# Two instruction counts in the model that orders a windowed-attention and gated-MLP kernel

## The chip, the cores and the metric

One core of one Trainium2 chip runs the whole kernel as one launch. The metric is the device time of one execution in microseconds; the time before is the median of three runs. The core has TensorE (PE, with its weight loads PEld), VectorE (DVE), ScalarE (ACT), GpSimd (POOL) and SyncE (SP, which issues nearly all DMAs here). Each engine works through its own list of instructions in order and waits on semaphores.

## What is computed

Attention over 8 batches and 8 heads of 576 tokens, with a window of 32 (heads 0 to 3) or a dilated window of 128 with step 4 (heads 4 to 7), and then a gated MLP on the 4608 tokens:

```python
scores = scale * np.matmul(q, k.transpose(0, 1, 3, 2))       # (8, 8, 576, 576), D = 64
mask_plain = (rel >= 0) & (rel < window)
mask_dil = (rel >= 0) & (rel < window * dilation) & (rel % dilation == 0)
attn = softmax(np.where(masks, scores, -1e9))
x = np.matmul(attn, v)                                       # to (4608, 512)
h = x @ w_in                                                 # (512, 2048)
out = (h * (1.0 / (1.0 + np.exp(-1.702 * h)))) @ w_out       # (2048, 512)
```

## The kernel before

**Work and stages.** Heads are taken in pairs: pair k is batch k // 4 and heads 2 (k % 4) and the next, so pairs 0 to 3 are batch 0 and pairs 2 and 3 of a batch are dilated. The first four pairs ("early" pairs) have a form of their own: `first_attention` (scores and softmax), `first_transposed` and `first_multiplied` (the product with v). The MLP is computed with every operand split into a high and a low part, in three matmuls for each product. Three groups (m0, m1, m2: the tokens of batches 0 to 2) go through `Group.up` and `Down`: for each of 16 chunks f of the hidden width, 12 matmuls into a bank `hp_m_f`, a tanh on ScalarE (line 855), a gating step on VectorE (line 856) that frees the bank, a copy to the high part `gh` (line 346), a subtraction to the low part `gl` (line 353), and 8 matmuls with `gh` (lines 784 and 785) and 4 with `gl` (line 788) into four accumulators `acc`. Three blocks of two groups each (p, q, r) then go through `up_` and `second_` matmuls (lines 992 and 1107). Each execution also decodes the weights, which come as 64-bit words, into high and low parts (`decode`): for each of the 32 pieces wi0 to wi15 and wo0 to wo15 a DMA of 512 KB and eight steps on ScalarE, VectorE and GpSimd (lines 396 to 406, 346, 353). This runs beside group m0.

**What sets the order.** The program doesn't write out an order. Each piece of work is handed to a `Plan` by `add`, with the engines that may run it and a cost on each, an urgency, what it reads and writes, and, for some pieces on TensorE, a `count`: the instructions that the piece has there. `Plan.placed` plays the program through with those costs: it takes, again and again, the engine that can start soonest and on it the most urgent piece, and chooses among engines that may run a piece. `Plan.ordered` does so four times, with due times worked out from the round before. The list that comes out is the order of every engine's instructions; the modelled times themselves are thrown away, and each piece then starts when its semaphores let it.

**The count.** `fetched` in `placed` holds that TensorE's program arrives in blocks of 256 instructions: the first edge is at instruction 193, the next ones at 449, 705, 961, 1217 and 1473, and nothing past instruction 1500 is modelled. At an edge the modelled engine waits until the next block is there, 4.2 or 6.1 us after it got to the edge before. Only pieces before instruction 1500 are moved by it directly; those are the four early pairs' scores and products, and the first matmuls of group m0.

**Fillers.** While `when < WARM` (60 us), the plan fills TensorE's modelled idle time with matmuls that nobody reads: 128x512 ones of bf16 (line 1249, two instructions each), and, before the next edge in the first 25 us, small ones (line 1253, four instructions each):

```python
small = min((193 + 256 * (len(blocks) - 1) - issued[0]) // 4 + 1, int((when - at - 0.1) / 0.045))
idle = max(0, int((when - max(at, 1.5) - 0.5) / size))
```

Their number hangs on the modelled idle time and on the instructions counted so far.

Of the kernel before, what the change touches and what calls it, by code (L numbers as in the profile page):

```python
# [43 lines left out]
PE, ACT, DVE, POOL, DMA = range(5)  # L44
# [4 lines left out]
class Plan:  # L49
# [9 lines left out]
    def add(self, costs, urgency, work, reads=(), writes=(), slack=0.0, count=0):  # L59

        i, after = len(self.ops), set()
        for k in reads:
            after.add(self.writer.get(k))  # L70
        for k in writes:
            after.add(self.writer.get(k))
            after.update(self.readers.get(k, ()))
        for k in writes:
            self.writer[k], self.readers[k] = i, []
        for k in reads:
            if k not in writes:
                self.readers.setdefault(k, []).append(i)
        self.ops.append((costs, (urgency, i), work, after - {None, i}, slack, count))
# [138 lines left out]
def tile_windowed_attention_then_gated_mlp(  # L218
# [19 lines left out]
    add = plan.add  # L238
# [7 lines left out]
    def bank(shape, tag, name):  # L246
        return ps.tile(shape, F32, tag=tag, name=name)
# [169 lines left out]
    FOUR = tuple(f"acc{j}" for j in range(NC))  # L417

    def lots(k):

        if 0 < k < NC:
            return f"first qk{k}", f"first v{k}"
        return "qk0", "v0"

    def load_qk(k):
        u, place = pairs[k], lots(k)[0]

        def work(e):
            if 0 < k < NC:
                flat = (None, late, main_x, left_x)[k]  # L430
            else:
                flat = temp([P, 2 * S], F32, "qk", f"qk_{k}")

            u["qk"] = flat[:, 0:2 * S]
            load(u["qk"], qk[k])

        add({DMA: 590}, (-9.0, -5.7, -4.7, -2.3)[k] if k < NC else 1.6 * k - 2.0, work, waits(k), (place, place + "l"))

    def load_v(k):
        u, place = pairs[k], lots(k)[1]  # L440

        def work(e):
            if k < NC:
                n = (QT if dilated(k) else QT + 1) * 2 * D
                flat = (None, late, main_x, left_x)[k][:, 2 * S:2 * S + n] if k else temp([P, n], F32, "v", f"v_{k}")
                u["v"] = flat.rearrange("p (s a d) -> p s a d", a=2, d=D)

                load(flat, first_v[k][:, 2 * D * (QT + 1) - n:])
                return
            flat = temp([P, 2 * NB * D], F32, "v", f"v_{k}")  # L450
            u["v"] = flat.rearrange("p (a s d) -> p a s d", a=2, s=NB)
            load(flat, vp[k - NC])

        add({DMA: 390 if k < NC else 328}, (-6.7, -6.7, -3.8, -1.6)[k] if k < NC else 1.6 * k - 0.3, work, waits(k),
            (place, place + "l"), (0.0, 4.0, 11.0, 14.0)[k] if k < NC else 0.0)
# [5 lines left out]
    def dilated(k):  # L461
        return k % NC >= NC // 2

    def turn(k):
        return k % (3 if FIRST * NC <= k < INNER else 2)

    def masked(k):

        return k < FIRST * NC

    def scores(k):
        u = pairs[k]
        u["sp"] = bank([P, 2, GT], "sp", f"sp_{k}")
        u["all"] = u["sp"][:, :, 0:QT * W].rearrange("p a (t w) -> p a t w", t=QT)
        u["box"] = [u["all"][:, a] for a in range(2)]
        if masked(k):
            for a in range(2):
                T.matmul(u["box"][a], ident, plain if not dilated(k) else classes if k < NC else mask, start=True,
                         stop=False, skip_group_check=True)
        for t in range(QT):  # L480
            for a, g in [(a, g) for a in range(2) for g in range(4 if k < NC or t < QT - 1 else 2)]:
                rows = slice(D * a, D * a + D)
                dst = u["box"][a][32 * g:32 * g + 32, t]
                at = ROW * g + 32 * t if k < NC else MID * (g % 2) + W * t + 32 * (g // 2)

                spans = [(0, W, at - 32)]
                if at + 32 > S:
                    spans = [(0, S + 32 - at, at - 32), (S + 32 - at, at + 32 - S, 0)]
                for w, n, first in spans:
                    T.matmul(dst[:, w:w + n], u["qk"][rows, at:at + 32], u["qk"][rows, S + first:S + first + n],  # L490
                             start=not masked(k), stop=True, tile_position=(D * a, 32 * g), skip_group_check=True)
# [28 lines left out]
    def softmax(k, urgency):  # L520

        y = turn(k)
        pr, sm, ct = prs[y], sms[y], cts[y]
        PR, SM, CT = (f"{n}{y}" for n in ("pr", "sm", "ct"))
        exponentials(k, urgency)
        add({DVE: 0.81}, urgency, lambda e: V.tensor_reduce(out=sm, in_=sets[y], axis=AX.X, op=ALU.add), (PR,), (SM,))
        inverse(k, urgency)
        for a in range(2):
            add({POOL: 0.85, DVE: -0.48}, urgency, lambda e, a=a: pair(
                e, pr[:, a], pr[:, a], sm[:, a, :, None].broadcast_to([P, QT, W]), ALU.mult), (SM,), (f"{PR}.{a}",))  # L530
        if k < NC:
            return
        for half in (0, 1):
            add({DVE: 0.42}, urgency, lambda e, half=half: V.transpose(  # L534
                out=ct[:, half].rearrange("p t a q -> p a t q"), in_=pr[:, :, :, 32 - 32 * half:64 - 32 * half]),
                (PR, f"{PR}.0", f"{PR}.1"), (f"{CT}.{half}",))

        for m in range(8):  # L540
            j, prev = m % 4, m // 4
            upper, second = j % 2, j in (1, 2)
            row = D * upper + 32 * (second != prev)
            col = 32 if second else 64 * prev
            tiles = slice(1 if j == 0 and prev else 0, QT - j // 2)
            to = slice(1, QT) if j == 3 and not prev else slice(0, tiles.stop - tiles.start)
            dst = bt[row:row + 32, to, :, col:col + 32]
            src = ct[32 * j:32 * j + 32, prev, tiles]

            def work(e, dst=dst, src=src):  # L550
                if e == DMA:
                    load(dst, src)
                else:
                    copy(e, dst, src)

            costs = {DMA: 82} if k < FIRST * NC else {ACT: 0.49, DVE: -0.33}
            add(costs, urgency, work, (f"{CT}.{prev}",), (f"bt.{m}",))

    def first_product(k):

        u = pairs[k]
        ct = cts[turn(k)].rearrange("p h t a q -> p (h t a q)").rearrange("p (a n) -> p a n", a=2)
        u["x"] = first_x[:, :, ROW * (k % 2):ROW * (k % 2) + ROW]
        for s in range(QT + 1):
            at, to = max(W * s // 2 - 32, 0), min(32 * s + 32, ROW)

            n = max(W * s - 32, 0)  # L570
            for g in range(4):
                if s == 0 and (g == 0 or dilated(k)):
                    continue
                for a in range(2):
                    T.matmul(u["x"][D * a:D * a + D, g, at:to],
                             u["v"][32 * g:32 * g + 32, s - 1 if dilated(k) else s, a],
                             ct[32 * g:32 * g + 32, a, n:n + to - at],
                             start=s == 0 or s == 1 and (g == 0 or dilated(k)), stop=s == QT, tile_position=(32 * g, D * a), skip_group_check=True)
# [88 lines left out]
    def first_attention(k):  # L667


        load_qk(k)  # L670
        load_v(k)
        add({PE: 1.5 if k else 2.3}, k - 1.0e5, lambda e: scores(k), (lots(k)[0],), ("sp", f"scores{k}"), count=180)
        softmax(k, k)

    def first_transposed(k):
# [5 lines left out]
    def first_multiplied(k):  # L681


        y = turn(k)
        add({PE: 1.4}, k - 1.0e5, lambda e: first_product(k), (lots(k)[1], f"ct{y}.0", f"ct{y}.1", f"scores{NC - 1}"),
            FOUR, count=184)
        drain_x(k, k)

    def attention(k, urgency):
# [516 lines left out]
    for c in range(NC):  # L1206
        first_attention(c)
        if c < 2:
            first_transposed(c)
        if c in (1, 2):  # L1210
            decode(c - 1, c + 1.3)
    for c in range(NC):
        first_multiplied(c)
        if c < 2:
            first_transposed(c + 2)
# [88 lines left out]
```

## Time and profile before

| | |
|---|---|
| median of 3 runs | 823.08 us (820.47 to 823.29) |
| the profiled execution, own time | 822.47 us |
| its span | 820.7 us |
| mean granted clock of TensorE | 0.999 of 2.4 GHz |
| PE busy | 806.5 us (98%) |
| PEld busy | 653.1 us (80%) |
| DVE, ACT, POOL busy | 665.0, 514.5, 330.5 us (81, 63, 40%) |

The sums below are made against the profiled execution's 822.47 us: the span of 820.7 us from its first to its last instruction, and 1.8 us around it. It lies 0.6 us under the median of the three runs. Matmuls overlap in the trace (one of 512 columns is shown for 0.39 us, and the next starts 0.23 us after it), so a busy PE may hide short waits; the idle time of PEld, and what ended it, shows them.

### The profile page before, as it was taken

How to read it: one execution, taken by the hardware profiler on the slowest of the kernel's cores; microseconds unless marked ns; L12 is line 12 of the kernel's file. 1: busy time of each engine (PE TensorE's matmuls, PEld its weight loads, DVE VectorE, ACT ScalarE, POOL GpSimd, SP SyncE). 2: the span in 40 equal slices, each digit the busy share in tenths (PEclk: the TensorE clock that was granted, in tenths of full speed). 3: DMA queues.
4: the chain of work that ended last, by engine and by line, in shares of the span. 5: the costliest groups of instructions: out<-in, count | busy, mean ns of one | idle time of the engine just before them, and what ended most of it. 6: DMA issues, size and time to landing. Idle time of an engine off the chain costs nothing.

```text
span 820.7 us, 18907 instructions
## 1 busy us (share of the span) xinstructions
PE 806.5 (98%) x7279; PEld 653.1 (80%) x7279; DVE 665.0 (81%) x1083; ACT 514.5 (63%) x982; POOL 330.5 (40%) x297
## 2 busy tenths in 40 slices
PE   7999999999999999999999999999999999999997
PEld 4677787888888888878888888888788888888886
DVE  6799989778788787798888999986679885867575
ACT  7998985667677767587766754556356534544340
POOL 3443417555746663222334555531215332112250
PEclk9999999999999999999999999999999999999999
DMA  9577659889667656796877878776565658675546
GB/s 354 172 242 211 182 176 302 289 287 317 201 213 251 201 190 228 251 314 229 264 251 252 284 217 287 234 255 187 174 207 189 204 185 278 201 223 158 178 151 182
DMA packets 109610, 188.13 MB, mean 229 GB/s; under 512 B 26448, under 2 KB 55376, under 8 KB 109520
## 3 DMA queue, kind: packets, MB, share of 16 engines
q1 hardware_dynamic: 109376, 186.78, 69.9%
q8 instruction: 58, 0.95, 0.5%
q14 instruction: 32, 0.26, 0.1%
q10 hardware_dynamic: 144, 0.13, 0.0%
HBM read 140.64 MB, written 45.09 MB: 226 GB/s over the span
## 4 chain that ended last, share of the span: by engine, by line
PE 90%; DVE 4%; DMA 3%; ACT 1%; issue 1%; SPq 0%; DVEq 0%; ACTq 0%
PE hp_m L847 14%; PE up_r L992 9%; PE up_q L992 9%; PE up_p L992 9%; PE second_p_Q L1107 5%; PE second_q_Q L1107 5%; PE second_r_Q L1107 5%; PE acc_m L784 5%; PE acc_m L788 5%; PE acc_m L785 5%; PE sp L490 3%; PE second_r_Z L1107 3%; PE second_p_Z L1107 3%; PE second_q_Z L1107 3%; PE second_R L1107 3%; PE av L593 2%
## 5 line engine op out<-in xcount | busy, mean ns | idle before, releaser
L353 POOL TENSOR_TENSOR arena<-arena 128x256 f32<-128x256 f32 (+3 forms) x96 | 99.5, 1051 | 131.7 <-DVE wo_kept L353 27.4
L847 PE MATMUL hp_m<-xs,wi_kept 128*128 128x512 f32 x504 | 128.6, 396 | 0.9 <-DVE arena L856 0.7
L847 PEld LDWEIGHTS hp_m<-xs,wi_kept 128*128 128x128 f32 x504 | 92.8, 188 | 22.8 <-DVE arena L856 2.2
L353 POOL TENSOR_TENSOR wo_kept<-arena,wo_kept 128x512 fp32r<-128x512 f32 x35 | 47.4, 1359 | 128.0 <-ACT wo_kept L346 90.3
L346 ACT ACTIVATE wo_kept<-arena 128x512 fp32r<-128x512 f32 x114 | 71.2, 630 | 39.6 <-PE second_r_Q L1107 11.0
L992 PE MATMUL up_r<-wi_kept,xs 128*128 128x512 f32 x336 | 85.3, 389 | 0.0
L992 PE MATMUL up_p<-wi_kept,xs 128*128 128x512 f32 x336 | 85.2, 391 | 0.0
L992 PE MATMUL up_q<-wi_kept,xs 128*128 128x512 f32 x336 | 84.1, 389 | 0.0
L992 PEld LDWEIGHTS up_r<-wi_kept,xs 128*128 128x128 f32 x336 | 63.1, 188 | 13.1
L992 PEld LDWEIGHTS up_q<-wi_kept,xs 128*128 128x128 f32 x336 | 63.1, 188 | 13.1
L992 PEld LDWEIGHTS up_p<-wi_kept,xs 128*128 128x128 f32 x336 | 62.7, 188 | 13.4
L353 POOL TENSOR_TENSOR wo_kept<-wi_last_units,wo_kept 128x512 fp32r<-128x512 f32 x26 | 35.9, 1380 | 86.1 <-ACT wo_kept L346 77.5
L353 DVE TENSOR_TENSOR wo_kept<-arena,wo_kept 128x512 fp32r<-128x512 f32 x86 | 62.4, 734 | 6.7 <-ACT wo_kept L346 6.0
L784 PE MATMUL acc_m<-gh,wo_kept 128*128 128x512 f32 x156 | 62.1, 398 | 0.6 <-ACT arena L346 0.5
L785 PE MATMUL acc_m<-gh,wo_kept 128*128 128x512 f32 x156 | 60.9, 391 | 0.0
L1013 ACT ACTIVATE arena<-arena 128x512 f32<-128x512 f32 x60 | 37.6, 628 | 34.9 <-DVE arena L353 30.5
L346 ACT ACTIVATE bt<-ct 32x256 f32<-32x256 f32 (+1 forms) x125 | 54.4, 435 | 7.2 <-DVE ct L534 3.9
L353 DVE TENSOR_TENSOR arena<-arena 128x512 f32<-128x512 f32 (+1 forms) x75 | 56.3, 756 | 2.8 <-ACT arena L346 1.7
L353 POOL TENSOR_TENSOR pr<-pr,sm 128x320 f32<-128x320 f32 x52 | 43.5, 849 | 26.4 <-DVE sm L518 22.6
L353 DVE TENSOR_TENSOR gl<-arena,gh 128x512 fp32r<-128x512 f32 x52 | 43.5, 836 | 7.5 <-PE acc_m L788 3.4
L346 ACT ACTIVATE wo_kept<-wi_last_units 128x512 fp32r<-128x512 f32 x48 | 30.2, 629 | 27.9 <-PE second_r_Z L1107 8.6
L1014 DVE SCALAR_TENSOR_TENSOR arena<-arena 128x512 f32<-128x512 f32 x60 | 46.6, 781 | 1.0 <-ACT arena L1013 0.5
(261 smaller groups left out, 1850.2 us busy)
## 6 DMA issues: line engine op xcount, KB each, us to landing
xs<-sums SPq DMA_DIRECT2D x168, 256.0 KB, 3.3
out_weights<-sums_o SPq DMA_DIRECT2D x63, 512.0 KB, 3.8
qk<-qk_dram SPq DMA_DIRECT2D x29, 576.0 KB, 4.3
xs<-sums_o SPq DMA_DIRECT2D x21, 512.0 KB, 3.5
v<-vp_dram SPq DMA_DIRECT2D x28, 320.0 KB, 4.3
sums<-arena SPq DMA_DIRECT2D x32, 256.0 KB, 3.1
sums_o<-arena SPq DMA_DIRECT2D x32, 256.0 KB, 3.0
arena<-wi_dram SPq DMA_DIRECT2D x15, 512.0 KB, 5.3
```

Of the source, the lines that this page charges most:

```text
L346: A.activation(dst, src, AF.Copy, scale=scale)
L353: (V if e == DVE else G).tensor_tensor(out=dst, in0=a, in1=b, op=op)
L490: T.matmul(dst[:, w:w + n], u["qk"][rows, at:at + 32], u["qk"][rows, S + first:S + first + n], start=not masked(k), stop=True, tile_positi ...
L593: T.matmul(u["x"][i][rows, at:at + last - first], u["v"][keys, a, m], bt[keys, m, a, first:last], start=(i, a) not in begun, stop=True, ti ...
L784: T.matmul(self.acc[j], w[:, 0, cols], high, start=f == 0, stop=False)
L785: T.matmul(self.acc[j], w[:, 1, cols], high, start=False, stop=False)
L788: T.matmul(self.acc[j], w[:, 0, P * j:P * j + P], low, start=False, stop=f == NF - 1)
L847: T.matmul(hps[f], wi(f)[:, st, cols], mv[:, c], start=c == 0 and k == 0, stop=c == NC - 1 and k == 2)
L992: T.matmul(self.banks[place], xs[:, slot, at:at + P], wi_kept[:, 2 * a + c, mv], start=fresh and c == 0 and k == 0, stop=c == 1 and k == 2 ...
L1013: add({ACT: 0.60}, -10.0, lambda e: A.activation(unit(tmp), src(), AF.Tanh, scale=0.851), need, own(tmp))
L1014: add({DVE: -0.70 if need[0][0] == "A" else 0.70}, -10.0, lambda e: V.scalar_tensor_tensor(out=unit(dst), in0=unit(tmp), scalar=1.0, in1=s ...
L1107: T.matmul(self.second[key], w[:, st, cols], mv, start=fresh and y == 0 and k == 0, stop=y == 1 and k == 2, skip_group_check=True)
```

## The change

An early pair's scores are counted as 172 instructions of TensorE in place of 180, and its product as 160 (dilated pairs) or 184 (the others) in place of 184. Nothing else is edited: no cost, no urgency, no operation.

```diff
-        add({PE: 1.5 if k else 2.3}, k - 1.0e5, lambda e: scores(k), (lots(k)[0],), ("sp", f"scores{k}"), count=180)
+        add({PE: 1.5 if k else 2.3}, k - 1.0e5, lambda e: scores(k), (lots(k)[0],), ("sp", f"scores{k}"), count=172)
...
         add({PE: 1.4}, k - 1.0e5, lambda e: first_product(k), (lots(k)[1], f"ct{y}.0", f"ct{y}.1", f"scores{NC - 1}"),
-            FOUR, count=184)
+            FOUR, count=160 if dilated(k) else 184)
```

By the code, scores of an early pair are 2 mask matmuls of bf16 with 2 instructions each and 42 matmuls of f32 with 4 each, which is 172; a product is 46 matmuls of f32 (184 instructions), or 40 (160) for a dilated pair, which leaves 6 out. So the counts now are those of the program. The pieces that the plan may put elsewhere are all others: of TensorE's pieces after the first some 900 change places by up to 30 positions or not at all, the last 390 or so stand as before, 209 pieces change their engine among DVE, ACT and POOL, and the fillers go from 31 large and 68 small ones to 29 and 70.

On TensorE, at 6.7 us, between the scores of pair 0 (`sp_188`) and those of pair 1, the fillers stand (`ones` the small, `ident` the large):

```order
 L490 MATMUL sp_188<-qk_127 32x48
 L490 MATMUL sp_188<-qk_127 32x16
-L1253 MATMUL idle<-ones 32x16 x19
+L1253 MATMUL idle<-ones 32x16 x21
 L1249 LDWEIGHTS ident
```

Two more small fillers, of four instructions each, stand ahead of everything that follows on TensorE.

On TensorE, at 36 to 41 us: the last three of the twelve matmuls of each of group m0's chunks 0 to 2 (they need the output of the last early pair), and then the first accumulation; before:

```order
L847 MATMUL hp_m_0_577<-xs,wi_kept 128x512 x3
L847 MATMUL hp_m_1_584<-xs,wi_kept 128x512 x3
L847 MATMUL hp_m_2_717<-xs,wi_kept 128x512 x3
L847 MATMUL hp_m_3_759<-xs,wi_kept 128x512 x3
L784 MATMUL acc_m_0_770<-gh_73,wo_kept 128x512
L785 MATMUL acc_m_0_770<-gh_73,wo_kept 128x512
```

and of the change:

```order
L847 MATMUL hp_m_0_577<-xs,wi_kept 128x512 x3
L847 MATMUL hp_m_1_584<-xs,wi_kept 128x512 x3
L847 MATMUL hp_m_2_714<-xs,wi_kept 128x512 x3
L784 MATMUL acc_m_0_766<-gh_73,wo_kept 128x512
L785 MATMUL acc_m_0_766<-gh_73,wo_kept 128x512
```

Three matmuls of chunk 3 no longer stand between chunk 2 and the accumulation; all twelve of chunk 3 now stand behind the twelve of the accumulation.

On ScalarE, at 33 to 40 us, from the copy of the last early pair's output (`xs_72<-first_x_96`) to the high part of chunk 0 (`gh0_73`), with decoding steps between (lines 396, 402, 403, and 346 into `wi_kept` or `wo_kept`); before:

```order
L346 ACTIVATE xs_72<-first_x_96 128x4x128
L402 ACTIVATE arena_78<-arena_78 128x512
L403 ACTIVATE arena_78<-arena_78 128x512
L402 ACTIVATE arena_78<-arena_78 128x512
L396 ACTIVATE arena_78<-arena_78 128x512
L855 ACTIVATE arena_78<-hp_m0_0_577 128x512
L346 ACTIVATE wi_kept_68<-arena_78 128x512
L402 ACTIVATE arena_78<-arena_78 128x512
L346 ACTIVATE gh0_73<-arena_78 128x512
```

and of the change:

```order
L346 ACTIVATE xs_72<-first_x_96 128x4x128
L346 ACTIVATE arena_78<-first_x_96 128x4x16
L402 ACTIVATE arena_78<-arena_78 128x512
L403 ACTIVATE arena_78<-arena_78 128x512 x2
L346 ACTIVATE wo_kept_70<-arena_78 128x512
L402 ACTIVATE arena_78<-arena_78 128x512
L855 ACTIVATE arena_78<-hp_m0_0_577 128x512
L396 ACTIVATE arena_78<-arena_78 128x512
L346 ACTIVATE wi_kept_68<-arena_78 128x512
L346 ACTIVATE gh0_73<-arena_78 128x512
```

Between the tanh of chunk 0 (line 855) and its high part `gh0` there now stand a step of line 396 and the copy into `wi_kept`, where there were the copy and a step of line 402.

## Rows read from the trace of the kernel before

**Rows 1.** The page, busy time by engine: microseconds, share of the span, instructions; and the granted clock of TensorE in 40 slices, in tenths.

```profile
PE 806.5 (98%) x7279; PEld 653.1 (80%) x7279; DVE 665.0 (81%) x1083; ACT 514.5 (63%) x982; POOL 330.5 (40%) x297
PEclk9999999999999999999999999999999999999999
```

**Rows 2.** Busy time of each engine by stage: stretch in us, its length, busy us and instructions of each engine, granted clock, DMA share, GB/s.

```profile
0.00:33.00 33.00, 25.55 (x854) 16.38 (x855) 22.66 (x53) 26.33 (x41) 14.73 (x23) 1.00 0.74 277
33.00:60.00 27.00, 26.67 (x287) 20.44 (x272) 24.94 (x43) 25.41 (x42) 11.53 (x9) 1.00 0.69 230
60.00:130.00 70.00, 69.73 (x800) 55.59 (x799) 64.52 (x108) 58.32 (x107) 25.33 (x21) 1.00 0.66 201
...
620.00:815.00 195.00, 194.98 (x858) 160.36 (x857) 141.48 (x210) 85.95 (x145) 58.49 (x43) 1.00 0.60 195
815.00:821.00 6.00, 0.97 (x5) 0.47 (x3) 1.77 (x4) 0.00 (x0) 0.00 (x0) 0.81 0.63 175
```

**Rows 3.** Who waited for whom, the weight loads from 33 to 130 us: total us, times, longest. "issue" is a wait that the profile puts down to nothing.

```profile
PEld hp_m L847 <- DVE arena L856: 0.9, 2, 0.7
PEld acc_m L784 <- ACT gh L346: 0.6, 1, 0.6
PEld hp_m L847 <- ACT wi_kept L346: 0.5, 1, 0.5
...
PEld hp_m L847 <- DVE wi_kept L353: 0.4, 1, 0.4
```

**Rows 4.** The same from 130 to 620 us.

```profile
PEld hp_m L847 <- DVE arena L856: 1.3, 2, 0.7
PEld acc_m L784 <- ACT arena L346: 0.9, 1, 0.9
PEld second_q_Q L1107 <- DMA out_weights<-sums_o: 0.7, 1, 0.7
PEld second_p_Q L1107 <- DMA out_weights<-sums_o: 0.6, 1, 0.6
```

**Rows 5.** Timeline at 92 us, one wait as the weight load and as the matmul show it: start us, us, engine, line, operation, and in brackets the idle time before and what ended it.

```profile
92.11 0.99 PEld L847 LDWEIGHTS hp_m<-xs,wi_kept 128*128 128x128 f32 x5 [0.69 <-DVE arena L856]
92.11 1.20 PE L847 MATMUL hp_m<-xs,wi_kept 128*128 128x512 f32 x4 [0.27 <-DVE arena L856]
```

**Rows 6.** Timeline of TensorE's matmuls from 8 to 30 us, merged; each matmul also has a weight load, so xN is 2 N instructions.

```profile
8.31 0.59 PE L1249 MATMUL idle<-ident 128*128 128x512 bf16 x1 [0.39 <-issue]
9.28 0.71 PE L478 MATMUL sp<-plain,ident 128*128 128x320 bf16 x2 [0.39 <-DVE pr L353]
10.17 1.44 PE L490 MATMUL sp<-arena 64*32 64x64 f32 x84 [0.17 <-DMA arena<-qk_dram]
...
17.97 0.86 PE L490 MATMUL sp<-arena 64*32 64x64 f32 x65
20.51 0.37 PE L490 MATMUL sp<-arena 64*32 64x64 f32 x19 [1.69 <-issue]
20.81 1.16 PE L575 MATMUL first_x<-ct,v 32*64 32x32 f32 x92
21.91 1.47 PE L1249 MATMUL idle<-ident 128*128 128x512 bf16 x6
23.82 0.32 PE L575 MATMUL first_x<-ct,arena 32*64 32x32 f32 x10 [0.45 <-ACT pr L514]
24.41 1.09 PE L575 MATMUL first_x<-ct,arena 32*64 32x32 f32 x82 [0.27 <-issue]
...
28.79 0.68 PE L575 MATMUL first_x<-ct,arena 32*64 32x64 f32 x41 [0.82 <-issue]
```

**Rows 7.** Timeline of TensorE and VectorE around the product of the last early pair.

```profile
30.91 1.47 PE L1249 MATMUL idle<-ident 128*128 128x512 bf16 x6
30.95 1.13 DVE L353 TENSOR_TENSOR xs<-first_x,xs 128x512 fp32r<-128x512 f32 x1 [0.89 <-ACT xs L346]
...
32.30 0.98 PEld L575 LDWEIGHTS first_x<-ct,arena 32*64 32x64 f32 x80 [0.42 <-DVE xs L353]
```

**Rows 8.** Timeline of ScalarE, VectorE and TensorE around the first accumulation.

```profile
37.77 0.60 ACT L855 ACTIVATE arena<-hp_m 128x512 f32<-128x512 f32 x1 [0.39 <-PE hp_m L847]
38.26 0.62 ACT L346 ACTIVATE wi_kept<-arena 128x512 fp32r<-128x512 f32 x1
38.40 0.69 DVE L856 SCALAR_TENSOR_TENSOR arena<-arena,hp_m 128x512 f32<-128x512 f32 x1 [0.33 <-ACT arena L855]
38.78 0.66 ACT L402 ACTIVATE arena<-arena 128x512 f32<-128x512 f32 x1
...
39.34 0.62 ACT L346 ACTIVATE gh<-arena 128x512 fp32r<-128x512 f32 x1
...
40.31 0.40 PE L784 MATMUL acc_m<-gh,wo_kept 128*128 128x512 f32 x1
```

**Rows 9.** Timeline of ScalarE: a step of line 396, and the start of the next.

```profile
26.19 1.39 ACT L396 ACTIVATE cell<-cell 128x512 f16<-128x512 f32 x1
...
27.30 0.72 ACT L402 ACTIVATE arena<-arena 128x512 f32<-128x512 f32 x1
```

**Rows 10.** Timeline of TensorE at 46 to 50 us: the first matmul of the accumulations of chunk 1 and of chunk 2, twelve matmuls apart.

```profile
46.38 0.50 PE L784 MATMUL acc_m<-gh,wo_kept 128*128 128x512 f32 x1
...
49.56 0.50 PE L784 MATMUL acc_m<-gh,wo_kept 128*128 128x512 f32 x1
```

## The prediction

> **What bounds the kernel now.** Read the page's busy times first: PE is busy for 806.5 of 820.7 us at full clock, DVE for 81%, ACT for 63% [rows 1]. Then the stages [rows 2]: from 33 us on PE is busy for all but some tenths in each, and from 620 to 815 us it never rests: 195.00 us for 858 matmuls, 0.227 us each. That pace is the floor of a large matmul here, and the change takes none away (the two large fillers that go and the two small ones that come lie in idle time). So only three things can move the time: the first 33 us, where PE is idle for 7.45 us [rows 2]; the waits from 33 to 620 us; and the end, 815 to 821 us, whose work is listed in the same order as before. The waits are read from the weight loads, since a matmul is shown longer than the step to the next: at 92 us the load shows 0.69 us of waiting and the matmul 0.27 [rows 5], so a listed wait costs TensorE some 0.42 us less than it says. That leaves little to win and no limit to what can be lost.
>
> **The change part by part.**
>
> *The stops for program blocks.* In the first 30 us TensorE stands four times for a reason that the profile calls issue: 0.39, 1.69, 0.27 and 0.82 us [rows 6]. From the stop at 20.51 us to the next there are 19 + 92 + 6 + 10 = 127 matmuls, 254 instructions, near the 256 of the plan's blocks. So they hang on the count of instructions, and the corrected counts are about something real. But only the plan's picture of them is corrected; the chip's stops stay at their instruction numbers. With two more small fillers (four matmul records) ahead of it, the stop in the scores of pair 3 comes 4 matmuls earlier, with 23 of them left, not 19; one more large filler later, 127 records on, the next stop leaves 87 of pair 1's product and not 82, and the one after that 45 of pair 2's and not 41. Each stop ends when its block is there, 3.90 and 4.38 us after the one before ended [rows 6], so only what is left behind the last one counts: 4 matmuls of 0.68/41 us, +0.07 us. At 8.31 us the stop now falls among the small fillers, with two large ones behind it, not one. Up to 0.59 us more stands there before the masks of pair 1, against 0.39 us of waiting that hides part of it, and the scores behind them wait for their DMA anyway until 10.17 us [rows 6]. From nothing to 0.2 us; I take nothing, because the DMA's row is the nearer one.
>
> The Trainium skill's page "Runtime: NRT & Kernel Launch" (section "Instruction fetch mechanics") says that program comes in blocks of 256 instructions and that crossing one is mostly hidden. Rows 6 agree with the size and not with the hiding. By the page the term above would be nothing in place of 0.07 us, and the third rival below could not be.
>
> *The fillers before the last early product.* Four large ones stand there where six stood [rows 7], and one is gone before pair 2's product. That is no gain: the weight loads of pair 3's product end a wait for VectorE at 32.30 us [rows 7]. VectorE's subtraction runs to 32.08 us, after ScalarE's copy of pair 2's output, and both come in the same place in the chain as before. The fillers hid nothing else. 0 us.
>
> *The first accumulation.* This is the place where the new order shows. Before, the accumulation of chunk 0 starts at 40.31 us, with `gh` ready at 39.34 + 0.62 = 39.96 us [rows 8], and three matmuls of chunk 3 ahead of it, which themselves waited for the decoded `wi_kept` (0.5 and 0.4 us by the loads) [rows 3]. Now nothing stands between chunk 2 and the accumulation, and ScalarE has a longer list before `gh`. From the tanh at 37.77 us it is 0.49 us to the next start [rows 8], then a step of line 396, 1.11 us from start to start [rows 9], then the copy to `wi_kept`, 0.52 us [rows 8], then `gh`, 0.62 us: 37.77 + 0.49 + 1.11 + 0.52 + 0.62 = 40.51 us. VectorE's gating step must be over by 39.89 us; before it ran until 39.09 us [rows 8], so 0.8 us of delay there is covered, and beyond that each microsecond counts in full. The accumulation starts 0.2 us later than before, and three matmuls that were done are still to do: 3 x 0.227 = 0.68 us. Together +0.88 us, and 0.07 us from above: +0.95 us.
>
> *What is given back.* The accumulation of chunk 2 starts at 49.56 us, chunk 1's at 46.38 [rows 10]; twelve matmuls take 12 x 0.227 = 2.73 us, so 0.45 us of it is no work of those twelve. One load there waits 0.6 us for `gh` [rows 3], which by the correction above is 0.2 to 0.6 us; I take 0.3 us. If TensorE comes 0.95 us later to it, and ScalarE is not also later, that wait is gone. So TensorE is 0.95 - 0.3 = 0.65 us behind at 50 us. Bounds: 0.2 us (all waits of this stretch are absorbed) to 1.2 us (none, and the early masks come 0.2 us later).
>
> *50 to 620 us.* The plan is made anew with the same costs and rules, so most instructions of ScalarE, VectorE and GpSimd change place. What before lost here is bounded by the listed waits [rows 3, 4]: hp behind the gating step 0.9 and 1.3 us, acc behind ScalarE 0.9, and two matmuls behind `out_weights` DMAs 0.7 and 0.6 us. That is 4.4 us by the loads in seven waits; less 0.42 us each, 1.5 us. I take 3 us as what is lost, between the two ends. The new order has waits of its own, in other places. Nothing in the rows says fewer or more, so I take the same: 0 us, from -3 us (none is left) to +3 us (twice as many).
>
> *From 620 us.* The list of TensorE is the same; 0 us.
>
> Sum: 822.47 + 0.65 = **823.1 us**, against a median of 823.08 us: no change that can be told.
>
> **The rivals.**
>
> *Slower: `gh` behind decoding, again and again.* Group m0 goes through 16 chunks while the weights are decoded, and ScalarE is busy for 25.41 of 27 us from 33 to 60 us and for 58.32 of 70 us after [rows 2]. If the new order puts a step of line 396 ahead of the high part in other chunks too, TensorE loses there what it loses at chunk 0, 0.88 us. Five more chunks would be 4.4 us and past 827.2 us; seven of the fifteen give 823.1 + 6.2 = 829.3 us. For it: that it happens at the first chunk, and that VectorE (64.52 of 70 us) has no room to step in. Against it: later chunks have twelve matmuls of the next chunk and twelve of the one before between a tanh and its use, some 5.5 us.
>
> *Faster: the waits go.* If the new order happens to have none of the 3 us from 50 to 620 us, and the front's loss is at its lower end of 0.2 us, it is 822.47 - 3 + 0.2 = 819.7 us. With the larger 4.4 us it is 818.3 us, the most that the rows leave. For it: the plan's start is now nearer to the chip's. Against it: the waits after 130 us lie far from the early pairs, and stand behind VectorE and DMAs, whose costs the change leaves alone.
>
> *The corrected counts do at the start what they say.* The plan now sees the stops where they are and could have put work into them. The four stops are 3.17 us [rows 6]; only those from 20.51 us lie in a row without other waits, and if the largest, 1.69 us, were filled or passed by, it would be 823.1 - 1.69 = 821.4 us. Against it: the same pieces stand on both sides of each stop in the new list, only fillers differ, and a filler can't bring a block earlier.
>
> **How the numbers follow.** Forecast 0.63 (own range 820.1 to 826.1 us: the 3 us either way), repeated delays behind decoding 0.20, waits gone 0.10, stops passed 0.07. A measurement of this kernel can tell about 0.5% from no change: 819.0 and 827.2 us about the median. Half of the waits-gone case lies under 819.0 us, and a little of the forecast, 0.06 in all; the slower case, all but its smallest sizes, and a tail of the forecast are 0.20; 0.74 is left for within. The range reaches down to the waits-gone case, 819.5 us, and up into the slower one, 828.5 us; that leaves out about 0.07 below and 0.13 above.
>
> **What would show it.** In the new profile the stops of some 0.4, 1.7, 0.3 and 0.8 us are still there in the first 30 us. Pair 3's product still starts at 32.3 to 32.5 us behind VectorE. The first accumulation starts at 40.4 to 40.8 us after a wait of over a microsecond for ScalarE's `gh`, with chunk 3 behind it. From 620 us on every row reads as before, shifted by one amount. If that accumulation starts by 39.5 us, the step on ScalarE is wrong; if PE's weight loads wait for `gh` in many chunks from 50 to 130 us, the slower rival is right; if the waits for other engines from 50 to 620 us sum by the loads to far from 4.4 us, the time goes with them.

## The result, and the profile after

The change is slower: 829.07 us (median of 6 runs, 826.89 to 831.74) against 822.83 us (6 runs of the kernel before, 820.47 to 823.67), a ratio of 1.0083, 95% interval 1.0065 to 1.0100. The forecast was 823.1 us and the range ended at 828.5 us. The profiled execution of the changed kernel took 831.59 us with a span of 829.9 us, 9.2 us more than the span before.

Busy time by engine, from the page, and then busy time by stage, in the columns of [rows 2], of the changed kernel:

```profile
PE 808.1 (97%) x7281; PEld 654.0 (79%) x7281; DVE 676.5 (82%) x1076; ACT 516.3 (62%) x992; POOL 327.5 (39%) x294
```

```profile
0.00:33.00 33.00, 25.15 (x866) 16.45 (x866) 23.73 (x53) 26.34 (x40) 12.34 (x21) 1.00 0.75 277
33.00:60.00 27.00, 25.27 (x256) 19.86 (x252) 26.93 (x46) 25.70 (x42) 7.75 (x6) 1.00 0.70 234
60.00:130.00 70.00, 69.90 (x664) 55.22 (x662) 63.95 (x107) 59.39 (x107) 23.97 (x22) 1.00 0.65 194
...
500.00:620.00 120.00, 115.45 (x500) 94.59 (x500) 94.39 (x135) 57.41 (x98) 36.49 (x26) 0.99 0.65 209
```

The stage from 500 us of the kernel before, which [rows 2] leaves out:

```profile
500.00:620.00 120.00, 119.73 (x528) 98.72 (x528) 96.03 (x140) 62.35 (x106) 38.46 (x28) 1.00 0.69 216
```

Two things differ from [rows 1, 2]. VectorE is busy for 676.5 us, not 665.0, with 7 instructions fewer: steps of the same kinds take longer. And one late stage has a hole: from 500 to 620 us TensorE idles for 4.55 us where it was 0.27. From 33 to 60 us it idles for 1.73 us where it was 0.33, and from 60 to 130 us it is as busy as before.

The waits of TensorE's matmuls from 130 us on (total us, times, longest) name the holes:

```profile
PE second_p_Q L1107 <- DVE arena L1131: 3.0, 1, 3.0
PE up_q L992 <- DVE arena L353: 1.5, 2, 1.3
PE hp_m L847 <- DVE arena L856: 0.9, 1, 0.9
PE second_r_Z L1107 <- DMA out_weights<-sums_o: 0.9, 1, 0.9
```

The first is at 499 us, the second at 554, the third at 234, the fourth at 818. Counted from the end of both traces, the matmul of the same number (the order differs, so it isn't the same one everywhere) stands 0.8 us later than before at 60 us, 0.5 later at 100, 0.2 earlier at 160 to 200, 1.3 later at 260, 1.4 at 480, 6.8 at 510, 8.4 at 560 and 9.1 at 815. So of the 9.2 us some 7 were lost in two places, 499 to 507 and 554 us.

**What happened at 499 us.** TensorE's timeline there (start, us, line, matmuls merged, and in brackets the idle time before):

```profile
499.23 0.86 PE L1107 MATMUL second_p_Q<-wo_kept,out_weights 128*128 128x512 f32 x3
503.04 0.97 PE L1107 MATMUL second_p_Q<-wo_kept,out_weights 128*128 128x512 f32 x3 [2.95 <-DVE arena L1131]
503.84 1.31 PE L992 MATMUL up_q<-wi_kept,xs 128*128 128x512 f32 x3
504.95 1.48 PE L1107 MATMUL second_p_R<-wo_kept,out_weights 128*128 128x512 f32 x3
506.23 1.42 PE L992 MATMUL up_q<-wi_kept,xs 128*128 128x512 f32 x3
507.49 0.84 PE L1107 MATMUL second_p_Q<-wo_kept,out_weights 128*128 128x512 f32 x3
```

It waits for VectorE's step of line 1131, which empties the bank. VectorE had no idle time. Its own timeline, and then GpSimd's:

```profile
498.29 0.68 DVE L1131 SCALAR_TENSOR_TENSOR arena<-second_p_Z,arena 128x512 f32<-128x512 f32 x1
498.89 1.82 DVE L1014 SCALAR_TENSOR_TENSOR arena<-arena 128x512 f32<-128x512 f32 x1
500.63 1.75 DVE L353 TENSOR_TENSOR wo_kept<-wi_last_units,wo_kept 128x512 fp32r<-128x512 f32 x1
502.31 0.68 DVE L1131 SCALAR_TENSOR_TENSOR arena<-second_p_Q,arena 128x512 f32<-128x512 f32 x1
```

```profile
495.52 3.39 POOL L353 TENSOR_TENSOR wo_kept<-arena,wo_kept 128x512 fp32r<-128x512 f32 x2 [1.91 <-PE up_q L992]
498.87 1.29 POOL L353 TENSOR_TENSOR arena<-arena 128x512 f32<-128x512 f32 x1
500.11 1.72 POOL L353 TENSOR_TENSOR wo_kept<-wi_last_units,wo_kept 128x512 fp32r<-128x512 f32 x1
```

Read the two side by side: the engines take turns. GpSimd starts at 498.87 and ends at 500.16; VectorE's step, shown from 498.89, ends at 500.71, 0.55 us after. GpSimd's next, shown from 500.11, ends at 501.83, 1.12 us after that; VectorE's next ends at 502.38, again 0.55 after. A step of about 0.68 us becomes one of 1.8. A third such step (1.78 us at 495.98) stands a little earlier. The steps with an operand in a PSUM bank (`second_p_Z` at 498.29 beside GpSimd's 3.39) keep their 0.68. Three holds of some 1.1 us make VectorE 3.3 us late, and TensorE waits 2.95. The Trainium skill's page "SBUF — State Buffer" (section "Who interferes with whom") says that a VectorE instruction with two inputs in SBUF and a GpSimd instruction that reads SBUF can't run together: the one issued second stands until the first is done. These rows agree, with 1.1 us for each turn of GpSimd.

The clock fell behind that wait, as the stages at 500 us show, in the columns of [rows 2]:

```profile
500.00:505.00 5.00, 2.05 (x8) 1.57 (x8) 5.00 (x7) 2.30 (x4) 1.83 (x2) 0.90 0.70 252
505.00:507.00 2.00, 2.00 (x6) 1.60 (x5) 2.00 (x4) 0.00 (x0) 0.00 (x0) 0.50 0.41 133
```

0.50 is the 1.2 GHz level. The nine matmuls from 503.84 to 507.49 us take 3.65 us; at the usual 0.227 us they would take 2.04. So 1.6 us went to the clock, on top of the 3.0 us of waiting, in this execution.

**The other places.** At 554 us the same picture: three VectorE steps of 1.77 to 1.78 us (548.03, 549.73, 551.43) beside GpSimd's three, then `up_q` waits 1.3 us. At 234 us VectorE's steps from 228.49 on take 1.2 to 1.4 us beside GpSimd, and the gating step, which was done at 232.9 us before, starts at 234.96: `hp_m` waits 0.93 us.

**The front**, TensorE's timeline (to be read against [rows 6, 7, 8]):

```profile
19.95 0.43 PE L490 MATMUL sp<-arena 64*32 64x64 f32 x23 [1.41 <-issue]
...
24.21 1.12 PE L575 MATMUL first_x<-ct,arena 32*64 32x32 f32 x87 [0.21 <-issue]
...
32.07 1.20 PE L575 MATMUL first_x<-ct,arena 32*64 32x64 f32 x80 [0.87 <-DVE xs L353]
40.54 0.50 PE L784 MATMUL acc_m<-gh,wo_kept 128*128 128x512 f32 x1 [1.57 <-ACT gh L346]
```

The stops with 23 and 87 matmuls left are there (1.41 and 0.21 us), and so is one of 0.37 us at 7.74 us. The fourth, which was to leave 45 of pair 2's product, is not: that product waits 0.69 us for ScalarE, and then runs through. The last product starts at 32.07 us, 0.2 to 0.4 us earlier than forecast. The accumulation starts at 40.54 us (forecast 40.51) after a wait of over a microsecond. That this met the forecast to 0.03 us is luck. The same lists were run once more (scores_alone, below), and there the stop in the scores of pair 3 ends 1.1 us later, and the accumulation starts as much later:

```profile
21.04 0.43 PE L490 MATMUL sp<-arena 64*32 64x64 f32 x23 [2.13 <-issue]
...
41.63 0.50 PE L784 MATMUL acc_m<-gh,wo_kept 128*128 128x512 f32 x1 [1.74 <-ACT gh L346]
```

By the weight loads from 33 to 130 us, in the columns of [rows 3], `gh` is waited for once:

```profile
PEld acc_m L784 <- ACT gh L346: 2.0, 1, 2.0
...
PEld hp_m L847 <- DVE arena L856: 1.3, 3, 0.5
```

### The profile page after: what moved, and what is told of

It reads as the page before. It is cut to its first block, busy times and chain, and to the rows that moved or that the text cites. A ratio compares the mean times of both kernels' runs of the same rounds, so it can differ in the third digit from the quotient of the medians.

```text
span 829.9 us, 18910 instructions
## 1 busy us (share of the span) xinstructions
PE 808.1 (97%) x7281; PEld 654.0 (79%) x7281; DVE 676.5 (82%) x1076; ACT 516.3 (62%) x992; POOL 327.5 (39%) x294
## 4 chain that ended last, share of the span: by engine, by line
PE 85%; DVE 7%; DMA 4%; ACT 2%; issue 2%; SPq 0%; DVEq 0%; ACTq 0%
PE hp_m L847 15%; PE up_r L992 9%; PE up_p L992 9%; PE up_q L992 6%; PE second_q_Q L1107 5%; PE second_r_Q L1107 5%; PE acc_m L784 5%; PE acc_m L788 5%; PE acc_m L785 5%; PE second_p_Q L1107 4%; PE sp L490 3%; PE second_q_Z L1107 3%; PE second_R L1107 3%; PE second_r_Z L1107 2%; PE second_p_Z L1107 2%; DMA out_weights<-sums_o 2%
## 5 line engine op out<-in xcount | busy, mean ns | idle before, releaser
L353 POOL TENSOR_TENSOR arena<-arena 128x256 f32<-128x256 f32 (+3 forms) x101 | 108.6, 1085 | 147.0 <-DVE arena L353 29.3
L346 ACT ACTIVATE wo_kept<-arena 128x512 fp32r<-128x512 f32 x108 | 67.3, 629 | 41.9 <-PE second_r_Q L1107 10.5
L992 PE MATMUL up_q<-wi_kept,xs 128*128 128x512 f32 x336 | 85.8, 393 | 1.5 <-DVE arena L353 1.5
L353 POOL TENSOR_TENSOR pr<-pr,sm 128x320 f32<-128x320 f32 x52 | 41.5, 813 | 61.0 <-DVE sm L518 59.7
L353 POOL TENSOR_TENSOR wo_kept<-wi_last_units,wo_kept 128x512 fp32r<-128x512 f32 x24 | 32.6, 1357 | 76.7 <-ACT wo_kept L346 76.7
L346 ACT ACTIVATE bt<-ct 32x256 f32<-32x256 f32 (+1 forms) x131 | 57.0, 435 | 5.1 <-DVE ct L534 1.7
L353 DVE TENSOR_TENSOR arena<-arena 128x512 f32<-128x512 f32 (+1 forms) x71 | 53.2, 759 | 1.9 <-ACT arena L346 0.8
L346 ACT ACTIVATE gh<-arena 128x512 fp32r<-128x512 f32 x59 | 37.4, 634 | 22.9 <-DVE arena L856 10.2
```

Of the source, the lines that this page charges most:

```text
L346: A.activation(dst, src, AF.Copy, scale=scale)
L353: (V if e == DVE else G).tensor_tensor(out=dst, in0=a, in1=b, op=op)
L992: T.matmul(self.banks[place], xs[:, slot, at:at + P], wi_kept[:, 2 * a + c, mv], start=fresh and c == 0 and k == 0, stop=c == 1 and k == 2 ...
```

## The experiments

TensorE's pieces are numbered by their place in the plan's list; piece 134 starts at about 97 us, 596 at 337, 786 at 471 and 903 at about 555 us. The variants that cut the list build both plans and join them, so that only the order and the engine of pieces differ. Line numbers in these stand 11 to 16 higher.

```diff
+FROM, CUT = (1, 0), 786
...
+        head, rest = (self.listed(warm_until, soon, c) for c in FROM)
+        at = [j for j, (i, e) in enumerate(head) if e == PE and i is not None and i >= 0][CUT - 1] + 1
+        done = {i for i, e in head[:at]}
+        order = head[:at] + [(i, e) for i, e in rest if i is not None and i >= 0 and i not in done]
```

`listed` makes the plan with the old counts (0) or the changed ones (1); FROM says whose list comes first, CUT where the other takes over.

**late_old** (the change's list to 471 us, then the old one) and **late_new** (`(0, 1), 786`: the old list, then the change's).

> The list of the change up to the 786th piece of TensorE (471 us in its trace), and from there the remaining pieces in the order of the list before. Theory (what is lost is lost from 471 to 560 us, where the changed order lets VectorE fall behind and TensorE waits for it): 823 to 825 us, as before but for about 1.4 us, and no wait of TensorE over 1 us between 471 and 620 us. Rival (the loss comes from the front and the decoding, and the late waits only show it): 828 to 830 us.

> The list before up to the 786th piece of TensorE (471 us), and from there the remaining pieces in the order of the change. Theory (late order): 826 to 830 us, with a wait of second_p_Q for VectorE near 498 us of 2 us or more. Rival (front): 822 to 824 us, no such wait.

Measured: late_old 831.82 us (830.13 to 834.17; ratio 1.0118, 1.0096 to 1.0141), late_new 826.39 us (824.08 to 827.99; 1.0044, 1.0025 to 1.0063), beside 821.87 us for the kernel before. late_old misses what was expected and tells nothing of the order: at the joint VectorE idles for 5.22 us and TensorE waits 4.6 us for it. late_new carries the late waits with it, though everything up to 471 us is as before:

```profile
PE second_p_Q L1118 <- DVE arena L1142: 1.7, 1, 1.7
PE up_q L1003 <- DVE arena L364: 1.3, 1, 1.3
```

Both of the waits at 499 and 554 us are there; the first is shorter, 1.7 us and not 3.0. So they belong to the late part of the list, and do not need the front.

**late_no_gpsimd** (the change's list, with those pieces that GpSimd has between 471 and 555 us, 28 (30 instructions), given to VectorE in the same place) and **scores_alone** (only the scores' count corrected; on every engine the instructions stand as in the change, so the product's count has no effect of its own once the other is right).

```diff
+FROM, CUT = (1, 1), (786, 903)
...
+        order = self.listed(warm_until, soon, 1)
+        at = [j for j, (i, e) in enumerate(order) if e == PE and i is not None and i >= 0]
+        first, last = (at[n - 1] for n in CUT)
+        order = [(i, DVE if e == POOL and first < j < last and DVE in ops[i][0] else e) for j, (i, e) in enumerate(order)]
```

> The list of the change, but the pieces that GpSimd had between the 786th and the 903rd piece of TensorE (some 28, 471 to 559 us) are VectorE's, at the same places. Theory (VectorE falls behind because single instructions take 1.7 to 1.8 us in place of 0.68 beside GpSimd): no VectorE instruction of line 353 or 1014 over 1 us in that stretch, the wait of second_p_Q under 1 us, 823 to 826 us. Rival (VectorE has too much to do there in this order, whoever does the rest): 28 more instructions of 0.6 us are 17 us more of its time, the waits grow, 830 us or more.

> Only the scores' count is corrected (172), the product's stays at 184 for all. The built order is the same as that of the change on every engine, so this is a second measurement of it: 827 to 831 us. If the waits of second_p_Q near 499 us and of up_q near 553 us hang on the order, they are there again, of like size; if they are chance of one execution, they are not.

Measured: late_no_gpsimd 824.98 us (823.81 to 825.66; 1.0035, 1.0023 to 1.0047), scores_alone 829.57 us (827.72 to 831.67; 1.0086, 1.0064 to 1.0108). The second repeats the change, down to its waits of 3.0, 1.7, 1.5 and 0.9 us, so these hang on the order and not on chance. The first lies 4.6 us under the second (4.2 by the ratios), with more work on VectorE and not less. Its VectorE at the same place, and its stages there:

```profile
496.16 0.68 DVE L1142 SCALAR_TENSOR_TENSOR arena<-second_p_Z,arena 128x512 f32<-128x512 f32 x1
496.76 0.68 DVE L1025 SCALAR_TENSOR_TENSOR arena<-arena 128x512 f32<-128x512 f32 x1
497.36 0.68 DVE L364 TENSOR_TENSOR wo_kept<-wi_last_units,wo_kept 128x512 fp32r<-128x512 f32 x1
497.97 0.69 DVE L1142 SCALAR_TENSOR_TENSOR arena<-second_p_Q,arena 128x512 f32<-128x512 f32 x1
```

```profile
495.00:505.00 10.00, 10.00 (x46) 8.13 (x45) 10.00 (x18) 3.11 (x6) 0.00 (x0) 1.00 0.94 298
545.00:560.00 15.00, 15.00 (x68) 12.42 (x67) 14.40 (x21) 8.15 (x15) 3.00 (x2) 1.00 0.64 211
```

The two steps that took 1.82 and 1.75 us take 0.68, the bank is emptied in time, TensorE has no hole and the clock stays up. That GpSimd is what held VectorE, and that this cost the late 4 to 5 us, is shown by it, with the control that follows. (Of the 128x512 steps with an operand in a PSUM bank, some 280 in this program, none takes over 0.73 us in the trace before or in that of the change; of those with both operands in SBUF, none that ran without GpSimd beside it takes over 0.73.)

**before_no_gpsimd**: the same edit on the old list (`(0, 0)`), as a control.

> The control for late_no_gpsimd: the list before, with GpSimd's pieces between the 786th and the 903rd piece of TensorE done by VectorE. Theory (what the edit gave the change, 4.6 us, is the wait that it removes there, and the list before has no such wait): within 1 us of before, 821 to 823 us. Rival (the edit is good for any order): 818 to 820 us. Third (VectorE gets too much): 824 us or more.

Measured: 822.53 us (820.92 to 824.83; 1.0001, 0.9989 to 1.0014; before 822.61). The edit is worth nothing by itself; it pays only where TensorE stood behind a held step.

**narrow_no_gpsimd**: late_no_gpsimd with `(786, 839)`, only up to 507 us, to part the two late waits.

> The change's list with GpSimd's pieces given to VectorE only between 471 and 507 us (14 pieces, half of those of late_no_gpsimd). Theory 1 (the 3.0 us wait at 499 us and the low clock behind it cost 4.3 to 4.6 us, the wait of 1.3 us at 554 us is a later one with a cause of its own, the same sort of instructions there): the first goes and the second stays, 825.0 + 1.3 = 826.3 us. Rival (the second wait follows from the lateness that the first left behind): the second goes too, 825.0 us. Rival (the low clock was not due to the wait): without the wait at 499 us matmuls between 500 and 507 us still stand 0.43 us apart, about 827.5 us.

Measured: 826.80 us (825.06 to 827.85; 1.0051, 1.0037 to 1.0064; before 821.92). Its waits from 130 us, and its stages at 500 us:

```profile
PE up_q L1003 <- DVE arena L364: 1.3, 1, 1.3
PE second_r_Z L1118 <- DMA out_weights<-sums_o: 1.1, 1, 1.1
PE hp_m L858 <- DVE arena L867: 0.9, 1, 0.9
```

```profile
500.00:505.00 5.00, 5.00 (x23) 4.12 (x23) 5.00 (x10) 1.16 (x2) 0.00 (x0) 1.00 0.97 325
505.00:510.00 5.00, 5.00 (x22) 3.82 (x22) 5.00 (x9) 1.31 (x3) 0.67 (x1) 1.00 0.95 293
```

The first late wait is gone, the second stays at its 1.3 us although TensorE came to it on time, and without the wait the clock doesn't fall. Both rivals are out, by the trace. What each wait is worth the times tell less well. By the ratios it is 1.0051 - 1.0035 for the second, 1.3 us, and 1.0086 - 1.0051 for the first with its slow stretch, 2.9 us; by the intervals of the ratios these stand within some 1.5 and 2.1 us. So the second alone isn't clear of nothing, and the first may well be the 4.6 us of the profiled execution. If it is less, the clock may not fall in each run: of the six runs of the change, the three with a mean clock of 0.998 or 0.999 took 826.89 to 829.04 us, the three with 0.995 to 0.997 took 829.09 to 831.74. That reading isn't tested by a run of its own.

**decode_new** (`(1, 0), 134`: the change's list to 97 us, then the old one), **mid_new** (`(1, 0), 596`: to 337 us) and **product_alone** (only the product's count corrected, which gives a third order).

> The list of the change up to the 134th piece of TensorE (97 us), and the list before from there: the front and half of the decoding alone. Theory (the front costs what the predicted chain says, and some is given back): 822.3 to 823.3 us against 821.9, a wait of acc for ScalarE's high part of 1.7 to 1.9 us near 38 us, and TensorE at 97 us within 0.5 to 1 us of before. Rival (the decoding is where most is lost): 826 us or more.

> The list of the change up to the 596th piece of TensorE (337 us), ahead of all work of the second block, and from there the list before. late_old cut in the midst of the second block's token sums, and VectorE idled 5.22 us there for a DMA and the copy behind it, so that run doesn't tell. Theory (471 to 560 us in the new order is where 5 us and more go): 822.5 to 825 us, no wait over 1 us after 337 us. Rival (what is lost late follows from the state that the first 337 us leave): 827 to 830 us, with waits over 1 us between 471 and 560 us in the old order too.

> Only the product's count is corrected (160 for the dilated pairs), the scores' stays at 180; a third list out of the same model. Theory (each new list is a new draw of waits at the second block, and the counts mean nothing by themselves): anything from 820 to 830 us, and where it is slower by over 3 us the profile has one or two waits of TensorE over 1 us behind VectorE between 471 and 560 us. Rival (correct counts are worse than wrong ones since they add to the front): within 1 us of before, since the scores' count, which moves the fillers and the first accumulation, is as before.

Measured, beside 822.61 us before: decode_new 825.12 (824.28 to 826.41; 1.0035, 1.0023 to 1.0048), mid_new 825.27 (823.82 to 828.30; 1.0034, 1.0019 to 1.0050), product_alone 824.54 (824.14 to 825.91; 1.0031, 1.0019 to 1.0042). None has a wait of over 1.0 us for another engine from 250 to 720 us, and they lose 2.5, 2.7 and 1.9 us. For decode_new (822.3 to 823.3 us) and mid_new (up to 825) that is more than was expected. decode_new has 1.0 us of small waits at its joint (99 to 105 us), so its loss isn't all the front's.

**front_order, drain_first, front_and_drain**: late_no_gpsimd with one edit each and with both. The first puts the decoding step of line 396 behind the first `gh` on ScalarE; the second puts VectorE's gating step at 232 us ahead of a subtraction and an addition.

```diff
+        step = order.pop(next(j for j, (i, e) in enumerate(order) if i == 144))
+        order.insert(next(j for j, (i, e) in enumerate(order) if i == 269) + 1, step)
...
+        late = [order.pop(next(j for j, (i, e) in enumerate(order) if i == n)) for n in (1325, 953)]
+        at = next(j for j, (i, e) in enumerate(order) if i == 1307) + 1
+        order[at:at] = late
```

> The list of late_no_gpsimd (the change's order, with GpSimd's pieces between 471 and about 555 us given to VectorE), with one more edit: the 1.36 us decoding step that stands ahead of the first gh on ScalarE's queue is put behind it. Theory 1 (the time lost is the sum of the waits seen, and a wait taken away gives back its length, unless a later wait takes it): the wait for the first accumulation falls from 1.9 us to about 0.6, so 823.9 us if nothing later takes it, but the lag of 1 us that it left had gone by 160 us in the change's profile, so as low a gain as 0 can stand: 824.0 to 825.0. Theory 2 (the rest of the loss is spread over many steps and no wait of the front is part of it): 825.0, the same as late_no_gpsimd (824.98).

> The list of late_no_gpsimd with one more edit: at 232 us VectorE drains hp before the last of the four subtractions that make xs and before one addition, where the change's order has it behind both. Theory 1 (a wait taken away gives back its length): the wait of 0.9 to 1.1 us of hp at 234 us goes and nothing of its size follows, 824.0 us. Theory 2 (the rest of the loss is spread over many steps): the wait goes and comes back as others, 825.0 us.

> The list of late_no_gpsimd with both edits, the decoding step behind the first gh and the drain first at 232 us. Theory 1 (the loss is the sum of the waits): 823.0 to 824.0 us, within 1.4 us of the kernel before. Theory 2 (the rest of the loss is spread): 825.0 us.

Measured, beside 821.92 us before: front_order 825.38 (825.05 to 825.77; 1.0037, 1.0025 to 1.0049), drain_first 825.60 (823.89 to 826.35; 1.0035, 1.0022 to 1.0048), front_and_drain 825.04 (823.29 to 827.39; 1.0035, 1.0024 to 1.0045).

front_order is a miss. The wait for the first accumulation is still 1.74 us. ScalarE's and VectorE's timelines show why:

```profile
38.65 0.58 ACT L868 ACTIVATE arena<-hp_m 128x512 f32<-128x512 f32 x1
40.15 0.63 ACT L359 ACTIVATE wi_kept<-arena 128x512 fp32r<-128x512 f32 x1 [0.93 <-DVE arena L366]
40.75 0.63 ACT L359 ACTIVATE gh<-arena 128x512 fp32r<-128x512 f32 x1
41.28 1.36 ACT L409 ACTIVATE arena<-arena 128x512 f16<-128x512 f32 x1
```

```profile
39.44 0.68 DVE L366 CUSTOM_DVE_ANT_0 arena<-arena 128x1024 uint16<-128x1024 uint16 x1
40.04 0.68 DVE L869 SCALAR_TENSOR_TENSOR arena<-arena,hp_m 128x512 f32<-128x512 f32 x1
```

The step was moved, and ScalarE then stands idle for 0.93 us until VectorE has decoded the next piece; VectorE's gating step, which `gh` needs, ends only at 40.72 us, 2.07 us after the tanh started; in the change it was 2.09. Both engines were late together, and to take one's work away gives nothing.

drain_first and front_and_drain do take the wait of 0.9 us at 234 us away, and in their traces nothing takes its place up to 500 us. The medians can't tell it: their intervals reach 1 us to either side, and the profiled execution of drain_first lost time to a low clock at 42 us (below).

## Why the prediction was wrong

**The step that failed is "50 to 620 us: 0 us, from -3 us to +3 us".** The profiled execution lost 0.9 us at 234 us, 3.0 and 1.6 at 499 to 507 us and 1.3 at 554 us there, 6.8 us, over twice the upper bound. That bound took the waits of the kernel before and doubled them. It took for granted that a new order has more or fewer waits of the size that the old one had, some 0.6 us. But three meetings of GpSimd with VectorE within 6.5 us, ahead of a bank that TensorE needs, make a wait of another size, 3 us. Long holds were there to be read in the trace before. From 130 to 620 us it has 12 VectorE steps of 128x512 over 1.5 us, and the change 17; for example, with no wait of TensorE behind them:

```profile
485.23 1.78 DVE L353 TENSOR_TENSOR wi_last_units<-wi_last_units,arena 128x512 f32<-128x512 f32 x1
...
488.65 1.77 DVE L353 TENSOR_TENSOR wo_kept<-wi_last_units,wo_kept 128x512 fp32r<-128x512 f32 x1
```

So what the new order brought is less the holds than their place. The plan itself knows of them: `port` in `placed` keeps GpSimd's pieces and some of VectorE's apart in the model's time. On the chip only semaphores set the start. That a new list drifts against the model in other places, and that the two engines meet where both drift together, is argued from this and was not traced. The prediction priced the counts, the stops and the queues, and left this coupling out; nothing in it says what happens when a VectorE step is held. Its last sign held: by the loads, the large matmuls' waits for other engines and DMAs from 50 to 620 us sum to some 11 us, not 4.4, and the time went with them.

**The first 50 us** were right in the mechanism of the accumulation: ScalarE's list ahead of `gh` took its terms to 0.06 us each. The text had VectorE's gating step covered by 0.8 us; it moved from 39.09 to 39.81 us, so the cover was all but used up, and front_order shows that ScalarE's list alone was not the limit. In size the agreement (0.6 us behind at 50 us, forecast 0.65) is in part luck, since the start itself varies. With the change's lists, the stop in the scores of pair 3 lasts 1.29 to 2.42 us in seven traces, and TensorE stands 0.5 to 2.2 us later at 50 us than in the profiled execution before, 1.2 in the mean. In the two other traces with the old list there it stands 0.6 and 0.7 us earlier. So the front costs nearer 1.7 us than 0.65, by few traces, and over the upper bound of 1.2. *What is given back* came later than forecast, by 160 us and not by 50. *The fillers* were priced at nothing and seem to have given 0.2 us: the last product now starts 0.05 us after VectorE's subtraction ends, where it was 0.22. *The stops* kept their place in the count of instructions, but one of the four was hidden by a wait. The rule in the Trainium skill's page "Runtime: NRT & Kernel Launch" (section "Instruction fetch mechanics"), that crossing a block is mostly hidden, again doesn't agree with the rows: 1.41 us at one of them; only the fourth crossing shows no stop.

**From 620 us: 0 us** was off by 0.9 us: at 818 us `second_r_Z` waits for an `out_weights` transfer, issued at 813.1 us, that took 6.2 us to land; the longest of the last four took 5.3 us before. The order there is unchanged, and the size differs from one variant to the next (none to 1.1 us).

**The rivals.** "`gh` behind decoding, again and again" named 829.3 us, which is near the time, but it is not what happened: `gh` was waited for once. "The waits go" and "the counts do at the start what they say" did not occur as told: the stops of 0.37, 1.41 and 0.21 us are still there. The fourth, 0.82 us, is gone, but TensorE is only 0.1 us ahead of the kernel before at 33 us.

**What stays open.** With the late waits taken away, 0.3% is left (1.0035 in late_no_gpsimd; 1.0031 to 1.0037 in six others). Its parts in the traces are a wait of 1.5 to 1.8 us at the first accumulation (in all but product_alone), of which the traces give most back later, and up to 1.1 us behind `out_weights` after 720 us; no trace with the old list shows either. Counted from the end of the trace, most of that loss is there before the late waits: at 480 us, four traces with the change's list up to there (after, scores_alone, late_no_gpsimd, narrow_no_gpsimd) stand 0.8 to 2.1 us later than the profiled execution before, and the two others with the old list 1.0 and 1.2 earlier. In the mean that is 2.0 us, of the 3.1 us that late_no_gpsimd's median shows. Removing the wait at 234 us, and moving ScalarE's step, didn't change the medians. Which steps make it up was not settled.

## What to carry to other kernels

An edit to a model that orders work is a new draw of the whole order: price it by the largest wait that a row of bad meetings of two engines can make, not by the waits that the present order happens to have. To bound that, look in the trace for instructions of one kind with two durations (here 0.68 and 1.8 us), see which other engine runs beside the long ones, and count how many of them stand in a row ahead of something that TensorE needs. Long steps with nothing waiting behind them cost TensorE nothing, as at 485 us before. Where something waits, move a few of the other engine's pieces away there: here that took some 4 us off, and on the order in which no one waited it cost nothing (1.0001).

Compare stretches over several traces, too. One trace of each kernel made the front look as forecast, and the others moved it by a microsecond.

## What the runs showed of the hardware

A VectorE step with both operands in SBUF stood behind GpSimd's in these traces (0.68 us alone, 1.75 to 1.82 us held), and one with an operand in a PSUM bank did not.

The clock fell to 1.2 GHz for some microseconds after a single wait in the middle of dense matmuls, and waits of like length differ in it: after 2.95 us of waiting it fell in the change, after 1.57 us (change) and 1.74 us (front_order) at the first accumulation it did not, and after 1.77 us in drain_first it did. There the stages read:

```profile
39.00:42.00 3.00, 1.23 (x6) 0.72 (x5) 2.97 (x6) 3.00 (x6) 0.00 (x0) 1.00 0.71 241
42.00:45.00 3.00, 3.00 (x10) 2.33 (x9) 3.00 (x7) 3.00 (x6) 0.00 (x0) 0.59 0.78 261
45.00:48.00 3.00, 3.00 (x13) 2.41 (x12) 3.00 (x8) 2.97 (x7) 0.00 (x0) 0.84 0.52 188
```

At the full clock thirteen matmuls fit into the 3 us from 42 us; ten started, so about 0.7 us went there, and more until 46 us. At 499 us the low clock cost half again what the profile lists for the wait.

The stop at one and the same place in the program isn't of one length: with the same list ahead of it, it lasts 1.29 us in one trace (late_no_gpsimd) and 2.42 in another (late_old). Behind it, seven large fillers took 1.69 us in three of the seven traces, with a granted clock of 1.00 from 20 to 24 us, and 2.46 to 2.94 us in the four others, with 0.57 to 0.77.
